# Feeding a float64 weight to a retention + FFN kernel piece by piece, with room for eight pieces, earlier conversions and a new order of the first chunks

## The chip, the cores and the metric

The kernel runs on one core of one Trainium2 chip. A core has a matrix engine (TensorE), a vector engine (VectorE), a scalar engine (ScalarE), a general engine (GpSimd) and an engine that here only issues transfers (SyncE); each works through its own queue in order. The metric is the device time of one execution in microseconds (us). The kernel before takes 979.1 us, the median of three runs (978.93 to 979.91).

## The reference

```python
# attention: q, k, v of shape (8, 8, 576, 64), float32
scores = scale * np.matmul(q, k.transpose(0, 1, 3, 2))
Dmat = np.where(rel >= 0, gamma[:, None, None] ** rel[None, :, :], 0.0)   # decay, one gamma per head
ret = scores * Dmat[None, :, :, :]
attn = np.matmul(ret, v)
# to x of shape (4608, 512), then a feed-forward layer with a squared relu
h = np.maximum(x @ w_in, 0.0)       # w_in  (512, 2048)
out = h * h @ w_out                 # w_out (2048, 512)
```

One thing in the inputs matters here: `w_in` and `w_out` are scaled by a float64 number and so come as float64. [...]the kernel converts both to float32 by integer operations on the two 32-bit words of each number.

## The kernel before

**Tiling.** Tokens are cut into chunks of at most 128 (576 = 4 x 128 + 64, so five chunks for each batch, 40 in all) for the retention, and into nine blocks of 512 for the feed-forward layer. A chunk goes through `turn` (transposes of q and k), `scores`, a masking, and `retain_a`, `retain_b`, `retain_c` (the outputs and the state that is carried from chunk to chunk); its result is copied to `xT`, the transposed input of the feed-forward layer.

**The weights.** `w_in` is cut into 16 pieces of 512 x 128: the list `pieces` holds a 128-wide column block m (0 to 7) and a half e of the hidden dimension. A piece is loaded as float64 (512 KB) into a raw buffer and converted by six steps (`round_parts`): `one` and `two` on VectorE take exponent and high fraction out of the high word (L234, L238), `beside` on ScalarE turns exponent (L242) and low word (L243) into floats, and `three`, `four`, `five` on VectorE put them together (L246, L249, L252). `w_in_parts` lines these steps up, from piece `N_ALONE` on with `one` and `two` of the next piece ahead of `three` of this one; `convert(count)` issues the next `count` of them. Where they are issued is written out by hand, between the parts of the first chunks and then in `ffn`.

**The loads.** The first two pieces are loaded singly (1 KB rows), the rest in pairs (2 KB rows, two neighbouring column blocks) into three pair buffers. `fetch_raw` loads the next ones if there is room; it is called by hand at first, and later by the last step of each conversion. All loads and stores apart from three at the start stand in the one queue of SyncE, in program order, also those of q, k and v and the stores of the hidden values (`g_dram`).

**Block 0.** The first block is multiplied without the Strassen scheme of the others, because it has only the pieces that are converted so far: step j (`first_in`, L699) takes piece j times the 512 tokens (eight matmul instructions of 512 columns), ScalarE applies the relu (L704), and the square (L707) is put into a list from which `some(2)` of a later step issues it on VectorE. The first `N_HALF` pieces are multiplied in two halves: with the first 256 tokens as soon as these are there, and with the other 256 when chunk 3 is done. The last four steps also issue sums of converted pieces for block 1 (L263 to L266). From chunk 5 on the loop calls `ffn(i - 1, 0)` and `ffn(i - 1, 1)`, which issue one, then two steps of block 0 for each chunk with six conversion steps between them. After block 0 the blocks 1 to 8 follow in Strassen form (L735, L1077), paced by the table `PACE`.

**Warm-up.** `warm(n)` (L862) issues matmuls on a constant whose result nobody reads; they keep TensorE occupied while it has no other work.

Of the kernel before, what the change touches and what calls it, by code (L numbers as in the profile page):

```python
# [10 lines left out]
U32 = mybir.dt.uint32  # L11
# [29 lines left out]
def kernel(  # L41
# [91 lines left out]
    def load(i, names="qkv"):  # L133
        b, ci, c0, cs = chunks[i]
        if i == 0:
            nc.sync.dma_start(dv, decays)
        got = loaded.setdefault(i, [None] * 3)
        for name, pool, src in (("q", ld3, q), ("k", ld5, k), ("v", ld4, v)):
            if name not in names:
                continue  # L140
            t = got["qkv".index(name)] = pool.tile([128, H, D], F32, tag=name, name=f"{name}_ld")

            issue = nc.scalar if i == 0 and name != "q" else nc.sync
            at = src[b, :, c0:c0 + cs, :].rearrange("h s d -> s h d")
            if name == "v":
                issue.dma_start(t[:cs], at)
            else:

                for e in range(2):
                    issue.dma_start(t[:cs, e * HP:(e + 1) * HP, :], at[:, e::2, :])  # L150
# [2 lines left out]

    pieces = [(0, 2 * mp + mm, e) for mp in range(N_MP) for e in range(2) for mm in range(2)]
    pieces += [(1, mq + mh * N_MQ, e) for mq in range(N_MQ) for mh in range(2) for e in range(2)]
    N_W1 = N_DF
    N_ALONE = 4
    N_HALF = 2  # L160
    stage = [W[5].rearrange("p (o s f) -> p o s f", o=4, s=NP),
             W[6][:, 0:3 * NP * 128].rearrange("p (o s f) -> p o s f", o=3, s=NP)]
    N_PAIR = 3
    raw_all = [W[4][:, j * 1024:(j + 1) * 1024] for j in range(3)]
    raw_one = [W[4 + j][:, 2048:3072] for j in range(2)]
    raw_two = [W[4 + j][:, 0:2048] for j in range(N_PAIR)]
    exp_all = [W[4 + j][:, 3072:3584] for j in range(3)]
    wide = moe_w_in.dtype != F32

    def raw_of(j):  # L170


        if j >= N_W1:
            return raw_all[(j - N_W1) % 3].rearrange("p (n two) -> p n two", two=2)
        if j < 2:
            return raw_one[j].rearrange("p (c f two) -> p c f two", c=N_DM, two=2)
        t = raw_two[(j // 2 - 1) % N_PAIR].rearrange("p (c m f two) -> p c m f two", c=N_DM, m=2, two=2)
        return t[:, :, j % 2, :, :]

    def exp_of(j):  # L180
        return exp_all[j % 2] if j < N_W1 else exp_all[2 * (j % 2)]
# [4 lines left out]
    def piece_src(j):  # L186
        wi, m, e = pieces[j]
        f = (m + e * N_M) * 128
        return moe_w_out[f:f + 128, :].rearrange("p (c f) -> p c f", c=N_DM)

    def in_src(j, count):
        wi, m, e = pieces[j]
        f = (m + e * N_M) * 128
        return moe_w_in.rearrange("(c p) f -> p c f", p=128)[:, :, f:f + 128 * count]

    def piece_dst(j):
        wi, m, e = pieces[j]
# [5 lines left out]
    def as_dst(j, t):  # L203

        if pieces[j][0] == 0:
            return t
        return t.rearrange("p (o s f) -> p o s f", o=2, s=2)

    def fetch_w(j):
        if j < len(pieces) and wide:  # L210
            to = raw_all[(j - N_W1) % 3].bitcast(I64).rearrange("p (c f) -> p c f", c=N_DM)
            nc.sync.dma_start(to, piece_src(j))

    def fetch_in(j, count):
        if not wide:
            return
        to = (raw_one[j] if count == 1 else raw_two[(j // 2 - 1) % N_PAIR]).bitcast(I64).rearrange("p (c f) -> p c f", c=N_DM)
        nc.sync.dma_start(to, in_src(j, count))

    def round_parts(j):
        first = pieces[j][0] == 0
        at = (lambda t, w: t[:, :, :, w]) if first else (lambda t, w: t[:, :, w])
        lo, hi = (at(raw_of(j).bitcast(U32), w) for w in range(2))
        frac = at(raw_of(j), 0)
        scale = exp_of(j).rearrange("p (c f) -> p c f", c=N_DM) if first else exp_of(j)
        exp = scale.bitcast(U32)
        t = piece_dst(j)  # L230
        bits = t.bitcast(U32)

        def one():
            nc.vector.tensor_scalar(exp, hi, 20, 0x7FF, op0=ALU.logical_shift_right, op1=ALU.bitwise_and)  # L234

        def two():

            nc.vector.tensor_scalar(bits, as_dst(j, hi), 0xFFFFF, 0x100000, op0=ALU.bitwise_and, op1=ALU.bitwise_or)  # L238

        def beside():  # L240

            nc.scalar.activation(exp, exp, AF.Relu, bias=exp_bias[:, 0:1], scale=2.0 ** 23)  # L242
            nc.scalar.activation(frac, lo, AF.Copy, scale=2.0 ** -52)  # L243

        def three():
            nc.vector.scalar_tensor_tensor(t, bits, 2.0 ** -20, as_dst(j, frac), op0=ALU.mult, op1=ALU.add)  # L246

        def four():
            nc.vector.tensor_tensor(t, t, as_dst(j, scale), op=ALU.mult)  # L249

        def five():
            nc.vector.scalar_tensor_tensor(bits, as_dst(j, hi), 0x80000000, bits, op0=ALU.bitwise_and, op1=ALU.bitwise_or)  # L252

        if not wide:
            if pieces[j][0]:
                return [lambda: nc.sync.dma_start(t.rearrange("p o s f -> p (o s) f"), piece_src(j))] + [lambda: None] * 5
            return [lambda: nc.sync.dma_start(t, in_src(j, 1))] + [lambda: None] * 5
        return [one, two, beside, three, four, five]

    def sum_w_in(mp):  # L260
# [51 lines left out]
    def fetch_raw(count):  # L312

        for _ in range(count):
            j = n_raw[0]
            if j < N_W1 and (j < 2 * N_PAIR + 2 or n_made[0] >= j - 2 * N_PAIR + 2):
                count = 1 if j < 2 else 2
                fetch_in(j, count)
                n_raw[0] += count


    def w_in_parts():
# [33 lines left out]
    load(1, "qk")  # L356
    fetch_raw(1)
    load(1, "v")
    load(2)
    fetch_raw(1)  # L360

# [457 lines left out]
    def ffn(i, half):  # L819

        gone[0] += chunks[max(0, min(i, N_CH - 1))][3] / 2
        if half == 2:
            gone[0] += chunks[min(i + 1, N_CH - 1)][3] / 2
        if steps and steps[0][0] == 0:

            move(6)
            for f in (step, lambda: convert(6)) if half else (lambda: convert(6), step):
                f()
            if half and steps and steps[0][0] == 0:
                step()  # L830
                convert(6)
            return
        if not behind:
            behind.append((gone[0] - HALF, done[0]))
        points = behind + [p for p in PACE if p[0] > behind[0][0]]
        want = points[-1][1]
        for (x0, y0), (x1, y1) in zip(points, points[1:]):
            if gone[0] < x1:
                want = y0 + (y1 - y0) * (gone[0] - x0) / (x1 - x0)
                break  # L840
        count = max(1, int(want) - done[0])
        while steps and count:
            held[0] = half != 1 and count <= (1 if half else 2)

            if half == 2:
                due = sum(m[0] <= i + 2 for m in moves)
                move(max(2, min(4, -(-due // (count - 1)))) if count > 1 else 0)
            else:
                move(4 if half and len(moves) > 8 else 3 if half else 2 if count > 1 else 0)
            busy[0] = len(flips) > 0  # L850
            for f in flips[:1]:
                f()
            del flips[:1]
            step()
            count -= 1
        held[0] = busy[0] = False


    def warm(count):
        t = ps_f.tile([128, 512], F32, tag="f", name="idle_ps")  # L860
        for _ in range(count):
            nc.tensor.matmul(t[:, 0:256], lhsT=idle, rhs=idle[:, 0:1].to_broadcast([128, 256]), start=True, stop=True)  # L862
# [17 lines left out]
    turn_in(0, (0,))  # L880
    turn_out(0)
    load(3)
    warm(1)
    scores(0)
    turn(1)
    fetch_raw(1)
    retain_a(0)
    scores(1)
    scale_q(2, nc.gpsimd)
    retain_b(0)  # L890
    retain_c(0)
    load(4)
    fetch_raw(2)
    convert(2)
    warm(1)
    retain_a(1)
    convert(1)
    warm(1)
    retain_b(1)
    retain_c(1)  # L900
    load(5)
    convert(3)
    turn(2, (0, 0))
    warm(2)
    scores(2)
    scale_q(3, nc.gpsimd)
    convert(2)
    first_in(0, (0,))
    retain_a(2)
    convert(1)  # L910
    retain_b(2)
    retain_c(2)
    load(6)
    convert(3)
    first_in(1, (0,))
    turn(3)
    warm(1)
    scores(3)
    scale_q(4, nc.gpsimd)
    convert(3)  # L920
# [1 line left out]
    early.close()  # L922
    ps_t[0] = first.enter_context(tc.tile_pool(name="ps_t", bufs=1, space=PS))
    turn(4)
    convert(3)
    retain_b(3)
    retain_c(3)
    load(7)
    fetch_raw(1)
    step()  # L930
    step()
    scores(4)
    convert(6)
    scale_q(5, nc.gpsimd)
    step()
    convert(6)
    for i in range(N_EARLY + 1, N_CH + 1):
        if i > N_ONE:
            move(C, i)
# [288 lines left out]
```

## Time and profile before

| | before |
|---|---|
| device time, median of 3 | 979.1 us |
| span of the profile | 973.0 us |
| TensorE busy | 951.0 us (98%) |
| VectorE busy | 783.2 us (80%) |
| ScalarE busy | 337.3 us (35%) |
| GpSimd busy | 135.0 us (14%) |
| TensorE's waits over 60 ns to 112 us | 13.4 us in 15 waits |
| `w_in` loads | two of 512 KB, seven of 1024 KB |

The profile comes from one execution, in which a hardware profiler records each instruction's start and end. A line such as `96.74 3.70 PE L699 MATMUL h_ps<-room,w ... x8 [0.17 <-DVE w L252]` reads: at 96.74 us from the start, for 3.70 us, TensorE (PE) ran eight matmuls of source line 699, which write the tile `h_ps` and read `room` and `w`; before them it sat idle for 0.17 us, and what ended this was the VectorE (DVE) instruction of line 252 that writes `w`. ACT is ScalarE, POOL GpSimd, SP SyncE. `PEclk` or "granted clock" is the share of the full TensorE clock that the chip grants.

### The profile page before, as it was taken

The numbers are of one execution on the slowest core, as the hardware profiler recorded it, in microseconds if no ns is written. First come the engines' busy times: TensorE is split into PE (matmuls) and PEld (weight loads), VectorE is DVE, ScalarE is ACT, GpSimd is POOL, SyncE is SP. The second block draws the span as 40 slices with busy tenths as digits, with TensorE's granted clock in tenths as the row PEclk, the third lists the DMA queues.
The fourth block names the chain that finished last, engine by engine and source line by source line (L and its number), as shares of the span: only waits on it lengthen the run. The fifth ranks groups of instructions, "written<-read, shape, count | busy, mean of one in ns | idle before, by whom it ended". The sixth has DMA issues, their size and how long they took to land. (4 is left out here: it accounts for less than half of the span.)

```text
span 973.0 us, 23644 instructions
## 1 busy us (share of the span) xinstructions
PE 951.0 (98%) x10004; PEld 849.6 (87%) x10004; DVE 783.2 (80%) x1445; ACT 337.3 (35%) x808; POOL 135.0 (14%) x121
## 2 busy tenths in 40 slices
PE   8799899999999999999999999999999999999998
PEld 6545588888888888878888899999999999999998
DVE  3698689988889887978876597888888787787876
ACT  3345276765765766656631000000000000000000
POOL 3311143222232122221210000000000000000000
PEclk9999899999999999999999999999999999999999
DMA  9966386686757876766158967445364454524241
GB/s 229 215 201 171 88 202 182 170 258 204 187 158 213 243 190 189 208 199 185 61 223 325 360 245 265 171 158 185 109 206 152 159 193 176 198 100 173 88 174 44
DMA packets 167034, 181.40 MB, mean 186 GB/s; under 512 B 116752, under 2 KB 123920, under 8 KB 160272
## 3 DMA queue, kind: packets, MB, share of 16 engines
q1 hardware_dynamic: 164832, 179.37, 59.3%
q8 instruction: 78, 1.28, 0.5%
q10 hardware_dynamic: 2096, 0.52, 0.2%
q14 instruction: 28, 0.23, 0.1%
HBM read 109.36 MB, written 70.52 MB: 185 GB/s over the span
## 5 line engine op out<-in xcount | busy, mean ns | idle before, releaser
L735 PE MATMUL h_b<-room,w 128*128 128x256 f32 x768 | 183.5, 382 | 2.1 <-DVE room L754 1.8
L438 ACT COPY qk<-flip 32x256 f32<-32x256 f32 x416 | 167.4, 402 | 6.2
L735 PEld LDWEIGHTS h_b<-room,w 128*128 128x128 f32 x768 | 144.2, 190 | 24.0 <-DVE room L754 3.0
L1077 PE MATMUL o_b<-w,room 128*128 128x128 f32 x1168 | 144.4, 275 | 0.2 <-DVE room L1029 0.2
L1077 PEld LDWEIGHTS o_b<-w,room 128*128 128x128 f32 x1168 | 137.2, 192 | 0.4 <-DVE room L1029 0.4
L735 PE MATMUL h_a<-room,w 128*128 128x256 f32 x512 | 122.4, 381 | 2.2 <-issue 2.2
L1077 PE MATMUL o_c<-w,room 128*128 128x128 f32 x1008 | 123.0, 275 | 0.0
L735 PE MATMUL h_c<-room,w 128*128 128x256 f32 x512 | 121.7, 380 | 0.0
L1077 PEld LDWEIGHTS o_c<-w,room 128*128 128x128 f32 x1008 | 117.7, 192 | 0.0
L735 PEld LDWEIGHTS h_a<-room,w 128*128 128x128 f32 x512 | 96.3, 190 | 16.0 <-issue 2.6
L735 PEld LDWEIGHTS h_c<-room,w 128*128 128x128 f32 x512 | 96.7, 190 | 13.3
L1091 ACT COPY r<-o_a 128x128 f32<-128x128 f32 x53 | 14.1, 265 | 271.7 <-PE o_a L1077 236.0
L1077 PE MATMUL o_a<-w,a 128*128 128x128 f32 x688 | 85.7, 275 | 0.0
L752 POOL TENSOR_TENSOR room<-room 128x512 f32<-128x512 f32 x32 | 35.8, 1119 | 337.2 <-ACT room L751 337.2
L1077 PEld LDWEIGHTS o_a<-w,a 128*128 128x128 f32 x688 | 81.2, 192 | 0.1
L742 DVE SCALAR_TENSOR_TENSOR room<-room 128x512 f32<-128x512 f32 x96 | 70.6, 735 | 3.3
L699 PE MATMUL h_ps<-room,w 128*128 128x512 f32 (+1 forms) x144 | 62.0, 577 | 8.6 <-DVE w L252 7.9
L401 POOL TENSOR_TENSOR q_ld<-q_ld,dv 128x512 f32<-128x512 f32 (+1 forms) x39 | 47.3, 1212 | 91.9 <-DMA q_ld<-in_q_dram 91.8
L594 PEld LDWEIGHTS x_ps<-qk,v_ld 64*64 64x64 f32 x1152 | 43.9, 134 | 16.8 <-issue 14.3
L699 PEld LDWEIGHTS h_ps<-room,w 128*128 128x128 f32 x144 | 27.1, 197 | 35.2 <-issue 25.5
L594 PE MATMUL x_ps<-qk,v_ld 64*64 64x64 f32 x1152 | 54.9, 223 | 2.7 <-issue 1.1
L515 POOL TENSOR_TENSOR v_ld<-v_ld,dv 128x512 f32<-128x512 f32 (+1 forms) x40 | 53.0, 1325 | 6.7 <-DMA v_ld<-in_v_dram 6.7
(105 smaller groups left out, 1348.8 us busy)
## 6 DMA issues: line engine op xcount, KB each, us to landing
g_dram<-room SPq DMA_DIRECT2D x32, 1280.0 KB, 5.7
a<-g_dram SPq DMA_DIRECT2D x30, 1024.0 KB, 5.7
room<-g_dram SPq DMA_DIRECT2D x15, 1024.0 KB, 5.8
w<-w_dram SPq DMA_DIRECT2D x7, 1792.0 KB, 9.9
out_dram<-room SPq DMA_DIRECT2D x17, 512.0 KB, 3.3
q_ld<-in_q_dram SPq DMA_DIRECT2D x64, 128.0 KB, 5.6
w<-in_moe_w_out_dram SPq DMA_DIRECT2D x16, 512.0 KB, 4.3
k_ld<-in_k_dram SPq DMA_DIRECT2D x62, 128.0 KB, 5.1
```

The lines of the kernel that those rows point to most:

```text
L401: engine.tensor_tensor(t, t, dv[:cs, :, NCH + ci:NCH + ci + 1].to_broadcast([cs, H, D]), op=ALU.mult)
L438: nc.scalar.copy(*moves.pop(0)[2:])
L515: nc.gpsimd.tensor_tensor(vs[:cs], vs[:cs], dv[:cs, :, ci:ci + 1].to_broadcast([cs, H, D]), op=ALU.mult)
L594: return [lambda hp=hp, e=e, b=b: nc.tensor.matmul(x_at(hp, e, b, h), lhsT=s["vs"][rows(h), head(hp, e), :], rhs=s["ret"][rows(h), e, hp, ...
L699: nc.tensor.matmul(p.rearrange("p h t -> p (h t)"), lhsT=w[:, c, :], rhs=xT[0][:, c, lo * HT:hi * HT], start=(c == 0), stop=(c == N_DM - 1))
L735: nc.tensor.matmul(p[:, mm, :], lhsT=w[:, c, :], rhs=xs[n][right][:, c, :], start=(j in OPENS and mm == 0 and c == 0), stop=(j in CLOSES a ...
L742: nc.vector.scalar_tensor_tensor(t, t, 0.0, t, op0=ALU.max, op1=ALU.mult)
L752: nc.gpsimd.tensor_tensor(g["A11"], g["A11"], g["A11"], op=ALU.mult)
L1077: nc.tensor.matmul(p, lhsT=s["lefts"][left][:, m, :], rhs=w_out[j][:, m, WO_SLOT[right], :], start=(i in OPENS and m == 0), stop=(i in CLO ...
L1091: nc.scalar.copy(r[:, 0, 0:128], p)
```

## The change

The change alters the feeding of `w_in` and the hand-written order of the first chunks:

- Each piece is loaded singly, in 1 KB rows, and there is room for eight raw pieces instead of two single ones and three pairs. The order of the pieces follows: both halves e of a column block come one after the other. A fetch may go out when the piece eight places earlier is converted.
- The loads stand sooner in the queue: the second piece ahead of chunk 2, the third ahead of chunk 3, two more ahead of chunk 4, and three ahead of chunk 5.
- Conversion starts sooner (three steps before `scores(1)`) and runs two pieces ahead of block 0 when the loop begins. `N_ALONE` goes from 4 to 3, and three pieces instead of two are multiplied in halves. Four of the calls of `warm` among the first chunks are left out.
- In `beside`, the low word is converted ahead of the exponent.
- Step 3 of block 0 is issued ahead of the loop; to make up for it, the first chunk of the loop issues one step less.

```diff
-    pieces = [(0, 2 * mp + mm, e) for mp in range(N_MP) for e in range(2) for mm in range(2)]
+    pieces = [(0, m, e) for m in range(N_M) for e in range(2)]
...
-    N_ALONE = 4
-    N_HALF = 2
+    N_ALONE = 3
+    N_HALF = 3
...
-    N_PAIR = 3
-    raw_all = [W[4][:, j * 1024:(j + 1) * 1024] for j in range(3)]
-    raw_one = [W[4 + j][:, 2048:3072] for j in range(2)]
-    raw_two = [W[4 + j][:, 0:2048] for j in range(N_PAIR)]
+    N_RAW = 8
+    raw_all = [W[4 + j // 3][:, (j % 3) * 1024:(j % 3 + 1) * 1024] for j in range(N_RAW)]
...
+            nc.scalar.activation(frac, lo, AF.Copy, scale=2.0 ** -52)
             nc.scalar.activation(exp, exp, AF.Relu, bias=exp_bias[:, 0:1], scale=2.0 ** 23)
-            nc.scalar.activation(frac, lo, AF.Copy, scale=2.0 ** -52)
...
-            j = n_raw[0]
-            if j < N_W1 and (j < 2 * N_PAIR + 2 or n_made[0] >= j - 2 * N_PAIR + 2):
-                count = 1 if j < 2 else 2
-                fetch_in(j, count)
-                n_raw[0] += count
+            if n_raw[0] < min(N_W1, n_made[0] + N_RAW):
+                fetch_w(n_raw[0])
+                n_raw[0] += 1
...
     load(1, "v")
+    fetch_raw(1)
     load(2)
     fetch_raw(1)
...
-            if half and steps and steps[0][0] == 0:
+            if half and i > N_EARLY and steps and steps[0][0] == 0:
...
     load(3)
+    fetch_raw(2)
     warm(1)
     scores(0)
     turn(1)
-    fetch_raw(1)
     retain_a(0)
+    convert(3)
     scores(1)
     scale_q(2, nc.gpsimd)
     retain_b(0)
     retain_c(0)
     load(4)
-    fetch_raw(2)
+    fetch_raw(3)
     convert(2)
-    warm(1)
     retain_a(1)
-    convert(1)
-    warm(1)
+    convert(4)
     retain_b(1)
     retain_c(1)
     load(5)
     convert(3)
-    turn(2, (0, 0))
-    warm(2)
+    first_in(0, (0,))
+    turn(2)
+    convert(3)
+    first_in(1, (0,))
     scores(2)
     scale_q(3, nc.gpsimd)
+    retain_a(2)
     convert(2)
-    first_in(0, (0,))
-    retain_a(2)
-    convert(1)
     retain_b(2)
     retain_c(2)
     load(6)
+    convert(1)
+    turn(3)
     convert(3)
-    first_in(1, (0,))
-    turn(3)
-    warm(1)
+    first_in(2, (0,))
     scores(3)
     scale_q(4, nc.gpsimd)
     convert(3)
...
     turn(4)
-    convert(3)
+    convert(2)
     retain_b(3)
     retain_c(3)
     load(7)
-    fetch_raw(1)
     step()
     step()
     scores(4)
     convert(6)
     scale_q(5, nc.gpsimd)
     step()
-    convert(6)
+    convert(3)
+    step()
+    convert(3)
```

More of the change, by code (lines that the diff above doesn't have):

```diff
@@ L170, in raw_of @@
     def raw_of(j):
[L173 to L178, printed above, removed]
+        return raw_all[j % N_RAW] if j < N_W1 else raw_all[(j - N_W1) % 3]
     def exp_of(j):
@@ L188, in piece_src @@
         f = (m + e * N_M) * 128
+        if wi == 0:
+            return moe_w_in.rearrange("(c p) f -> p c f", p=128)[:, :, f:f + 128]
         return moe_w_out[f:f + 128, :].rearrange("p (c f) -> p c f", c=N_DM)
[L191 to L194, printed above, removed]
     def piece_dst(j):
@@ L205, in as_dst @@
         if pieces[j][0] == 0:
-            return t
+            return t.rearrange("p (c f) -> p c f", c=N_DM)
         return t.rearrange("p (o s f) -> p o s f", o=2, s=2)
@@ L210, in fetch_w @@
         if j < len(pieces) and wide:
[L211 to L218, printed above, removed]
-    def round_parts(j):
[L224 to L229, printed above, removed]
+            nc.sync.dma_start(raw_of(j).bitcast(I64).rearrange("p (c f) -> p c f", c=N_DM), piece_src(j))
+    def round_parts(j):
+        words = raw_of(j).bitcast(U32).rearrange("p (n two) -> p n two", two=2)
+        lo, hi = words[:, :, 0], words[:, :, 1]
+        frac = raw_of(j).rearrange("p (n two) -> p n two", two=2)[:, :, 0]
+        exp = exp_of(j).bitcast(U32)
         t = piece_dst(j)
@@ L248, in four @@
         def four():
-            nc.vector.tensor_tensor(t, t, as_dst(j, scale), op=ALU.mult)
+            nc.vector.tensor_tensor(t, t, as_dst(j, exp_of(j)), op=ALU.mult)
         def five():
@@ L254, in round_parts @@
         if not wide:
-            if pieces[j][0]:
-                return [lambda: nc.sync.dma_start(t.rearrange("p o s f -> p (o s) f"), piece_src(j))] + [lambda: None] * 5
-            return [lambda: nc.sync.dma_start(t, in_src(j, 1))] + [lambda: None] * 5
+            to = t if pieces[j][0] == 0 else t.rearrange("p o s f -> p (o s) f")
+            return [lambda: nc.sync.dma_start(to, piece_src(j))] + [lambda: None] * 5
         return [one, two, beside, three, four, five]
```

## The prediction

> **What bounds the kernel now.** I read the stages first: TensorE's busy time by ten microseconds (stretch and length; busy us and instructions of TensorE, its weight loads, VectorE, ScalarE and GpSimd; granted clock; DMA share and GB/s).
>
> ```profile
> 30.00:40.00 10.00, 7.87 (x166) 6.42 (x161) 5.87 (x11) 3.42 (x8) 3.38 (x4) 1.00 0.92 223
> ...
> 60.00:70.00 10.00, 9.21 (x98) 4.41 (x98) 9.32 (x14) 5.30 (x11) 2.86 (x2) 1.00 0.83 210
> ...
> 100.00:110.00 10.00, 7.44 (x49) 3.65 (x48) 5.71 (x7) 1.34 (x3) 2.93 (x3) 0.66 0.07 27
> ...
> 140.00:150.00 10.00, 9.91 (x163) 8.56 (x162) 9.86 (x16) 6.91 (x16) 2.17 (x2) 1.00 0.29 82
> ```
>
> From 120 us on TensorE is full; over the whole span it is busy 951.0 of 973.0 us. What can be won lies in the first 112 us: the loads (DMA share near 1 to 45 us) and block 0, where VectorE, which converts `w_in` from doubles, is nearly as full as TensorE. The waits of TensorE to 125 us (total, times, longest) name the reason:
>
> ```profile
> PE h_ps L699 <- DVE w L252: 7.9, 7, 2.6
> ...
> PE x_ps L594 <- DVE qk L506: 1.0, 1, 1.0
> ...
> PE h_ps L699 <- ACT room L571: 0.7, 1, 0.7
> ```
>
> L252 is a conversion's last operation: TensorE waits seven times for a piece of `w_in`. The timeline of TensorE has the worst, piece 15:
>
> ```profile
> 96.74 3.70 PE L699 MATMUL h_ps<-room,w 128*128 128x512 f32 x8 [0.17 <-DVE w L252]
> ...
> 104.26 6.53 PE L699 MATMUL h_ps<-room,w 128*128 128x512 f32 x8 [2.56 <-DVE w L252]
> ```
>
> The same eight matmuls take 3.70 us in every other step and 6.53 here, since the clock was 0.50 from 103.16 to 109.98 us. So this wait cost 2.56 + 2.83 = 5.4 us. VectorE's timeline tells why piece 15 was late:
>
> ```profile
> 95.99 0.69 DVE L252 SCALAR_TENSOR_TENSOR w<-w,w 128x512 uint32<-128x512 uint32 x1
> 98.40 0.69 DVE L246 SCALAR_TENSOR_TENSOR w<-w,w 128x512 f32<-128x512 uint32 x1 [1.71 <-ACT w L243]
> 99.00 1.54 DVE L707 TENSOR_TENSOR room<-room 128x512 f32<-128x512 f32 x1
> 100.47 1.54 DVE L265 TENSOR_TENSOR w<-w 128x512 f32<-128x512 f32 x1
> 101.94 1.54 DVE L249 TENSOR_TENSOR w<-w,w 128x512 f32<-128x512 f32 x1
> 103.51 0.69 DVE L252 SCALAR_TENSOR_TENSOR w<-w,w 128x512 uint32<-128x512 uint32 x1
> ```
>
> L252 of piece 14 ends at 96.7. VectorE then waits 1.71 us for ScalarE, whose two conversions stand behind the Relu of step 13. Next come a square and a sum that belong to step 14, and only then L249 and L252 of piece 15; three operations take 1.54 us instead of 0.69 while GpSimd scales `v` (2.96 us at 99.96).
>
> **What the Trainium skill says.** "TensorE: Matmul & The Clock Gate", Part 1: the array runs at half rate after an idle window of about 3.4 us, in a free-running window of 3413 ns, and at full rate again after a busy one. The trace agrees on the period: 4.17 to 103.16 is 29.0 windows and the drop lasts 2.0. It does not agree that the window must be idle, as the windows below show. The same page (Architectural detail) has ScalarE and VectorE strictly FIFO; the chain above behaves so. "SBUF — State Buffer", Who interferes with whom: a VectorE operation with two SBUF inputs contends with a GpSimd one that reads SBUF; 0.69 against 1.54 agrees. "DMA: Bandwidth & Descriptors", Specifications, asks for 512 B or more per transfer for line rate; so single pieces (1 KB) should not be much worse than pairs (2 KB). In the trace a 1 KB packet took 51 to 53 ns in the median, a 2 KB one 84 to 89.
>
> **The change part by part.**
>
> (1) *Lead of the conversions.* Counting the steps handed to `convert`: before, 90 of 98 stand ahead of steps 12 and 13, 96 ahead of 14, and the last two (L249, L252 of piece 15) come after step 14. After: 92, 92, 98. So at the tightest places the lead grows from 4 to 6 operations, and piece 15's end is ahead of step 14's square and sum. It would run 98.4, 99.0, 99.7 on the old clock and end near 100.4, or 101.7 if GpSimd still meets it; step 14 ends at 100.4 and its small matmuls at 101.7. So the wait and the clock drop go: 5.4 us. The four smaller waits of the same kind between 50 and 97 us (0.17, 0.70, 0.79, 0.17) go too: 1.8 us.
>
> (2) *Does VectorE carry it?* From 45.07 to 104.26 us TensorE is busy 54.8 us of 59.2, VectorE 52.7, and VectorE waits 5.9 us for L243 (seven waits). It must end 3.9 us sooner for TensorE to run unbroken. It starts this stretch about one piece further on (2.6 us, from L234 of one piece to L234 of the next without waits), and with the fraction converted first, L246 need not wait for ScalarE's other operation (0.62 us from start to start, seven times, 4.3 us at most). 2.6 plus some of 4.3 is enough, by little. I take back 1.0 us for waits that stay (bounds 0 and 3.9).
>
> (3) *The first four chunks.* On landings: `w_in`'s second piece now goes ahead of chunk 2, a third ahead of chunk 3, two ahead of chunk 4. A piece needs 1.5 to 1.9 us (512 packets of 53 ns on 16 engines, and `v` of chunk 1 landed 1.2 us after the piece ahead of it), so `q` of chunk 2 lands near 14.5 instead of 12.4, `v` of chunk 3 near 23.3 instead of 21.3, `v` of chunk 4 near 30.5 instead of 29.2; chunk 5 as before within 1 us, since eight pieces are ahead of it in both. Their matmuls start later than that (retention of chunk 3 at 31.5 before), so no load ends a wait in my chain:
>
> ScalarE's copy of chunk 1 ends at 17.8; first half of step 0 (1.99) to 19.8; transposes of chunk 2 (0.7) to 20.5; first half of step 1 (1.97) to 22.5; scores (0.9) to 23.4; the masking is now bare (0.9, like the 0.99 at 31.48) to 24.3; retention (2.5, as 21.67 to 24.15) to 26.8; transposes (0.7) to 27.5; first half of step 2 (1.97) to 29.5; scores and mask (1.8) to 31.3; from there to the first second half 3.7 (31.48 to 35.20) to 35.0; two halves (3.7) to 38.7; scores (0.6), third half (1.9), step 3 (3.6), transposes of chunk 5 (0.8) to 45.6. The old kernel has the same work done at 48.7: 3.1 us won. The warm-up matmuls removed (3.2 us) filled idle time and give nothing back.
>
> (4) *The clock between 11 and 25 us.* Here I use the windows of 3.41 us that the clock events mark:
>
> ```profile
> 14.41:17.82 3.41, 2.76 (x91) 2.23 (x90) 0.64 (x1) 2.25 (x5) 1.15 (x2) 1.00 1.12 263
> ...
> 24.65:28.06 3.41, 1.67 (x8) 1.44 (x8) 1.86 (x4) 0.40 (x2) 0.54 (x1) 1.00 1.12 231
> ...
> 99.74:103.16 3.42, 1.96 (x42) 1.13 (x40) 3.42 (x3) 1.34 (x3) 3.19 (x3) 1.00 0.24 84
> ```
>
> The window that cost the clock had 1.96 us busy, 1.26 of it small matmuls of the retention; 1.67 us of dense ones did not. The first of the three loses 0.74 us of warm-up and 0.7 of transposes and would have some 1.35 us, all small. I expect the clock to drop near 17.8 and to come back after one full window: 3.41 us at half speed, 1.7 us lost (bounds 0 and 3.4).
>
> (5) *Small things.* Seven more DMA issues at about 0.4 us on SyncE, whose queue has room; the fetches of pieces 8 to 15 go out when five to eight pieces are made, and their old data are long read. Singles cost 0.4 us of transfer more per two pieces, beside other work. After block 0 the program is the same, and TensorE is full.
>
> Sum: 3.1 - 1.7 + 1.8 + 5.4 - 1.0 = 7.6 us; 979.1 - 7.6 = 971.5.
>
> **The rivals.** A: the clock holds in the early part (full rate from 4.17 to 103.16 in the old profile speaks for it, the windows against): 9.3 us, 969.8. B: VectorE is the bound at the end of block 0; the cycle from 87.67 to 104.26 has 14.70 us of VectorE against 13.86 of TensorE, so piece 15 is late again and the clock drops there. Only 3.1 - 1.7 + 1.8 and some 0.6 of the last wait are won: 975.3. Against it: the lead carries over from the cycles before, where VectorE has 12.1 of 13.5. C, slower: the later loads do end waits (2 us lost where I won 3.1), the early clock drop lasts two windows (3.4), and of the 7.2 us of waits only half go: +1.8, 980.9. DMA near 1.0 to 45 us speaks for it; chunk 3's 8 us of slack against.
>
> **How the numbers follow.** Forecast 0.44, A 0.29, B 0.14, C 0.13. The range leaves out C and the best of A: 967.5 to 976.5. Faster 0.86, the same 0.03 (between B and C), slower 0.11.
>
> **What would show it.** Step 15 starts within 1 us of the matmuls before it and takes 3.7 us at clock 1.00; L249 and L252 of piece 15 stand ahead of the square of step 13 or 14. The waits of L699 for L252 fall from 7.9 to under 2 us. Step 4 starts near 45.6 to 47.5 (old: 50.5). A half-rate window shows near 18 to 21 us. I am wrong if the early chain waits for `q`, `k` or `v`, if that drop lasts longer, or if VectorE reaches 100% in block 0 and TensorE still waits.

## The result, and the profile after

The changed kernel takes 967.7 us (median of 4 runs, 967.0 to 970.1) against 979.5 us of the kernel before in the same session: a ratio of 0.9882, 95% interval 0.9862 to 0.9902. The forecast was 971.5, with a range of 967.5 to 976.5. In the sessions of the experiments the kernel before had medians of 977.3 to 978.9 over 11 to 37 runs, so the gain is nearer 10 than 12 us (e5, which takes as long as the changed kernel, was 10.0 us under the kernel before in its own session).

The spans of the two profiles are 973.0 and 966.2 us. The waits of TensorE in the first 125 us come first (who waited for whom; total, times, longest, in us):

```profile
PE x_ps L571 <- issue: 2.5, 1, 2.5
PE x_ps L571 <- DVE qk L483: 2.5, 3, 1.0
...
PE h_ps L676 <- issue: 0.9, 1, 0.9
...
PE h_ps L676 <- DVE w L231: 0.3, 1, 0.3
```

Lines 676 and 231 are the old 699 and 252. The 7.9 us of waits for converted pieces are down to 0.3. What stands on top is new: "issue", a wait for nothing that the profile shows, and the masking (L483). The end of block 0 on TensorE, and piece 15 on VectorE, answer to the lines shown of before:

```profile
93.24 7.13 PE L676 MATMUL h_ps<-room,w 128*128 128x512 f32 x16
101.57 3.70 PE L676 MATMUL h_ps<-room,w 128*128 128x512 f32 x8
```

```profile
98.17 0.69 DVE L225 SCALAR_TENSOR_TENSOR w<-w,w 128x512 f32<-128x512 uint32 x1 [1.43 <-ACT w L221]
98.96 0.69 DVE L228 TENSOR_TENSOR w<-w,w 128x512 f32<-128x512 f32 x1
99.69 0.69 DVE L231 SCALAR_TENSOR_TENSOR w<-w,w 128x512 uint32<-128x512 uint32 x1
100.30 1.55 DVE L684 TENSOR_TENSOR room<-room 128x512 f32<-128x512 f32 x1
```

Steps 13 and 14 run back to back, and step 15 starts without a wait and takes 3.70 us where it took 6.53. Piece 15 is done at 100.4, ahead of the square that GpSimd slows to 1.55 us. The early part looks otherwise. Here are two lines of TensorE, and then its windows between clock events (stretch, length; busy us of TensorE, weight loads, VectorE, ScalarE, GpSimd; clock; DMA share, GB/s):

```profile
17.05 0.26 PE L571 MATMUL x_ps<-qk,v_ld 64*64 64x64 f32 x1 [2.54 <-issue]
...
20.66 3.78 PE L676 MATMUL h_ps<-room,w 128*128 128x256 f32 x8 [0.67 <-ACT room L548]
```

```profile
12.68:16.09 3.41, 0.99 (x42) 0.72 (x31) 3.27 (x6) 1.21 (x3) 1.36 (x2) 1.00 1.31 227
16.09:19.50 3.41, 1.98 (x62) 1.79 (x65) 1.30 (x3) 1.55 (x3) 1.06 (x1) 0.50 0.97 253
19.50:22.92 3.42, 2.75 (x25) 2.13 (x18) 1.75 (x3) 0.86 (x2) 1.47 (x1) 0.50 0.85 178
22.92:26.33 3.41, 3.41 (x22) 2.41 (x21) 0.77 (x2) 1.19 (x3) 1.06 (x1) 0.50 1.16 307
47.23:101.57 54.34, 54.34 (x634) 27.98 (x632) 47.45 (x79) 26.72 (x50) 7.74 (x7) 1.00 0.62 176
```

After a window with 0.99 us of work the clock is at half for three windows, and step 0's first half takes 3.78 us in place of 1.99. Step 3 and the transposes behind it end at 51.4 us; the old kernel had come as far at 48.7. From there TensorE is full without a break (last line). So the first 51 us lost 2.7 us, and the stretch to the end of block 0 won 8.2 (62.1 against 53.9), which puts the end of block 0 at 105.3 where it was at 110.8. The rest, from there to the end of the span, took 862.2 us before and 860.9 after.

### The profile page after: what moved, and what is told of

Same layout as the page of the kernel before. It is cut to its first block, busy times and chain, and to the rows that moved or that the text cites. A ratio compares the mean times of both kernels' runs of the same rounds, so it can differ in the third digit from the quotient of the medians.

```text
span 966.2 us, 23674 instructions
## 1 busy us (share of the span) xinstructions
PE 948.0 (98%) x10002; PEld 851.0 (88%) x10002; DVE 783.2 (81%) x1447; ACT 338.0 (35%) x808; POOL 134.4 (14%) x121
## 5 line engine op out<-in xcount | busy, mean ns | idle before, releaser
L729 POOL TENSOR_TENSOR room<-room 128x512 f32<-128x512 f32 x32 | 35.9, 1121 | 336.4 <-ACT room L728 336.4
L571 PEld LDWEIGHTS x_ps<-qk,v_ld 64*64 64x64 f32 x1152 | 44.3, 135 | 19.4 <-issue 16.1
L676 PEld LDWEIGHTS h_ps<-room,w 128*128 128x128 f32 x152 | 29.1, 199 | 24.4 <-issue 19.6
```

Of the source, the lines that this page charges most:

```text
L571: return [lambda hp=hp, e=e, b=b: nc.tensor.matmul(x_at(hp, e, b, h), lhsT=s["vs"][rows(h), head(hp, e), :], rhs=s["ret"][rows(h), e, hp, ...
L676: nc.tensor.matmul(p.rearrange("p h t -> p (h t)"), lhsT=w[:, c, :], rhs=xT[0][:, c, lo * HT:hi * HT], start=(c == 0), stop=(c == N_DM - 1))
L729: nc.gpsimd.tensor_tensor(g["A11"], g["A11"], g["A11"], op=ALU.mult)
```

## The experiments

Five rounds each, beside runs of the kernel before on the same chip; the ratio compares with those. Where two altered kernels are compared below, their medians can come from different sessions and chips, so such differences can be off by 2 or 3 us.

| run | median us (runs) | ratio to before, 95% interval |
|---|---|---|
| e1 kernel before again | 977.2 (22) | 0.9997, 0.9984 to 1.0010 |
| e2 changed, three warm-ups put back | 962.3 (5) | 0.9853, 0.9834 to 0.9872 |
| e3 before, with the lead alone | 972.1 (7) | 0.9960, 0.9932 to 0.9988 |
| e4 changed, without the lead | 974.1 (15) | 0.9964, 0.9947 to 0.9980 |
| e5 changed, exponent first | 967.6 (5) | 0.9895, 0.9874 to 0.9915 |
| e6 new feeding alone | 976.1 (14) | 0.9985, 0.9971 to 0.9999 |
| e7 e2, second piece behind chunk 2 | 963.4 (5) | 0.9849, 0.9825 to 0.9874 |
| e8 e2, scores ahead of the half steps | 962.8 (4) | 0.9847, 0.9823 to 0.9870 |
| e9 before, wait for piece 15 filled | 972.2 (10) | 0.9951, 0.9935 to 0.9967 |
| e10 before, four warm-up calls left out | 976.8 (22) | 0.9988, 0.9974 to 1.0002 |
| e11 e7 with three parts moved | 963.7 (4) | 0.9862, 0.9839 to 0.9885 |
| e12 changed, four matmuls at 47 us | 969.0 (6) | 0.9901, 0.9878 to 0.9925 |

**e1: how steady is the kernel before?** No edit.

> The kernel before, unchanged, to see clock and span of several of its executions: its profile had a span of 973.0 us at a mean clock of 0.996, but its timed runs take 979 us. Theory (the free-running activity windows fall differently in each execution): executions near 973 us with one clock drop of 6.8 us, and others near 978 us with further or longer drops, at clocks of 0.990 or less. Rival (the profiled execution is simply not comparable): all spans near 978 us at the same clock of 0.996.

Its 22 executions span 972.5 to 978.4 us, at mean clocks of 0.998 down to 0.990. In the profiled one (977.3 us) the clock fell four times: 25.7 to 32.5, 35.9 to 42.7, 107.6 to 111.0 and 428.4 to 431.9 us. In the profile that the prediction rested on it fell once. All drops are whole windows of 3.41 us, and the window grid stands elsewhere in each execution. The theory holds as far as this shows it: one program, the same order, and up to 6 us between executions. The eight with a mean clock of 0.996 or more have spans of 972.5 to 975.6 us, the six with 0.991 or less 976.4 to 978.4. That it is the place of the grid which decides is read from two profiles only. The profile of before was one of the better executions, 2 us below the mean span of 975.3.

**e3 and e4: the lead of the conversions, alone and taken away.**

```diff
 # e3, on the kernel before
     step()
-    convert(6)
+    convert(8)
 # e4, on the changed kernel
     step()
-    convert(3)
+    convert(1)
```

> The kernel before with two more conversion steps ahead of the loop (8 in place of 6), nothing else: the lead at steps 12 to 14 is then that of the changed kernel. Theory (the lead alone removes the waits for L252 and the clock drop at 103 us): 6 to 7.5 us faster than before, ratio 0.993. Rival (the gain needs the pieces loaded and converted sooner): under 2 us faster, ratio 0.998 or more.

> The changed kernel with two conversion steps fewer ahead of the loop (1 in place of 3), so that the lead is that of the kernel before; loads, buffers and order of the first chunks as changed. Theory (lead): the waits of block 0 for L231 come back, that for piece 15 with a clock drop, 5 to 7 us slower than the changed kernel, ratio 0.994. Rival (loads and early order): as fast as the changed kernel, ratio 0.988.

Two conversion steps more make the old kernel 5.4 us faster by the medians, 3.9 by the ratio (interval 1.2 to 6.6); two fewer make the changed one 6.4 us slower, which leaves 3.4 us against the kernel before for all the rest of the change. The end of block 0 in e3 and in e4:

```profile
93.84 7.13 PE L699 MATMUL h_ps<-room,w 128*128 128x512 f32 x16
102.16 3.70 PE L699 MATMUL h_ps<-room,w 128*128 128x512 f32 x8
```

```profile
86.98 3.70 PE L676 MATMUL h_ps<-room,w 128*128 128x512 f32 x8 [0.47 <-DVE w L231]
...
107.75 3.70 PE L676 MATMUL h_ps<-room,w 128*128 128x512 f32 x8 [1.83 <-DVE w L231]
```

In e3 step 15 follows without a wait; in e4 the waits for L231 are back, 3.4 us of them behind step 3 where the changed kernel has none, though not the clock drop at step 15 in this execution. From the end of step 3 (52.7 us in e4, 50.8 in the changed kernel, ahead of the transposes) to its own end, block 0 takes 58.7 us in e4 and 54.5 in the changed kernel. In the kernel before it takes 62.1, or 59.2 without what the slow clock costs step 15. So in block 0 nearly the whole gain goes with the lead. (e4's profile was also 1.9 us later at the end of step 3, where the two programs are still the same; that is not the lead's.) e3 falls a little short of the 6 to 7.5 us expected, since two smaller waits for L252 (0.8 us each at 73.6 and 88.0) stayed and scores waited for a copy on VectorE (1.5 us at 50.0): with the lead alone VectorE is still a little late in the middle, and block 0 takes 57.8 us from step 3 on. The lead removes the waits fully only together with the rest of the change.

**e9: what a wait costs beside its length.**

```diff
 # the kernel before
                 turn(i)
+            if i == N_EARLY + 5:
+                warm(4)
             move(C, i)
```

> The kernel before with four warm-up matmuls just ahead of step 15, in the 2.6 us in which TensorE waits for piece 15; the wait itself stays. Theory (the wait has two costs, 2.6 us of idle time and a clock drop that a sparse window brings): no drop after 100 us, and the mean 1.5 to 3 us under the kernel before (the drop is one or two windows of 3.4 us, at half speed). Rival (the drop comes with any wait, or the clock is hidden there): no difference, under 0.7 us.

```profile
104.70 2.01 PE L862 MATMUL idle_ps<-w 128*128 128x256 f32 x8
107.44 3.67 PE L699 MATMUL h_ps<-room,w 128*128 128x512 f32 x8 [0.73 <-DVE w L252]
```

The wait is about as long as before (2.7 us), now filled for 2.0 us of it, and step 15 runs at full clock. The gain was 5.2 us and so more than expected. The trace has a reason for the surplus, another gap: the old kernel idles on "issue" for 2.2 us at 425.9 us, and e9 has no such gap. In the profiles of e1, e3 and e6, which have it too, it lay mostly in one window, left 1.1 to 1.7 us of work there, and a clock drop of one window followed. So between 2 and 4 us of the 5.2 (an estimate: the gap, and half a window) may have nothing to do with the wait for piece 15. See e12.

**e2 and e10: the warm-up matmuls.**

```diff
 # e2, on the changed kernel
     convert(2)
+    warm(2)
     retain_a(1)
     convert(4)
+    warm(1)
     retain_b(1)
 ...
     convert(3)
+    warm(1)
     first_in(0, (0,))
```

> The changed kernel with warm-up matmuls put back into three idle places between 12.7 and 20.7 us (two calls ahead of the retention of chunk 1, one inside it, one ahead of step 0). Theory (the clock dropped at 16 us because that window was sparse, and cost about 3 us): no drop before 110 us, 2 to 3.5 us faster than the changed kernel, ratio to the kernel before 0.985. Rival (the early part is bound by loads and instruction fetch, the clock is hidden): within 0.7 us of the changed kernel, ratio 0.988.

> The kernel before without the four calls of warm that the change leaves out (ahead of the retention of chunk 1, inside it, and ahead of the scores of chunks 2 and 3). Theory (these matmuls filled idle time but held the clock): a drop between 14 and 18 us in every execution, 2 to 5 us slower than before, ratio 1.003 or more. Rival (they only cost time, and the drops have other causes): the same or up to 1.5 us faster.

e2 is 5.4 us faster than the changed kernel by the medians (2.8 by the two ratios, 4.1 by the ratio of e5) and has the lowest median of all. Its executions ran at mean clocks of 0.996 to 1.000, those of the changed kernel at 0.991 to 0.995. In the one profiled the clock still fell once, at 16.2, for two windows in place of three; block 0 ended at 102.2 in place of 105.3. e10 went against the expected time: it is as fast as the kernel before. Its clock did what the theory says (mean 0.990 over 22 executions against 0.994; a drop at 17.4 us behind a window with 1.32 us of work), and block 0 ended at 117.1 us in its profile against 110.8 and 113.2. But here too the gap near 426 us had gone, and the stretch behind block 0 took 859.8 us in place of 862.2. With the gap moved at the same time, e10 does not tell what the four calls are worth.

**e12: the gap at 420 us.**

```diff
 # the changed kernel, ahead of the loop
     convert(3)
+    warm(4)
```

> The changed kernel with four warm-up matmuls just ahead of the loop, at 47 us, where TensorE is full and its clock is not in question: the same number of added instructions as in the run with three warm-ups put back. Theory (TensorE's idle time of 2.0 us near 420 us is an instruction fetch whose place depends on how many instructions stand ahead of it): that gap goes or shrinks to 0.7 us, which gives back the 1.7 us that the four matmuls cost; within 0.7 us of the changed kernel (967.7), with the clock drop at 16 us as before. Rival (the gap has to do with the state of block 5 there, and the warm-ups gave all of the 5.4 us through the clock): the gap stays at 1.8 to 2.3 us and the kernel takes 1.7 us more, 969.4.

In the changed kernel the gap reads:

```profile
419.82 1.35 PE L712 MATMUL h_a<-room,w 128*128 128x256 f32 x5 [1.99 <-issue]
```

In e12 it is gone, TensorE is full from 410 to 440 us, and there is one of 0.49 us at 361 us instead. Over all 14 profiles the gap goes by the number of matmul instructions: 10002 or 10004 give 1.8 to 2.3 us between 419 and 428 us (7 profiles), 10010 give 0.5 to 0.7 near 355 (5), 9994 and 10012 none over 0.15 us. So its place depends on how many instructions stand ahead.

That it is an instruction fetch the DMA records show. Every profile has 78 packets of 16 KB of instructions; in the changed kernel one runs from 417.20 to 418.27 us, and the gap ends 1.55 us after it. The same holds for all 35 idle times on "issue" over 0.12 us in the 14 profiles: each ends 1.3 to 1.8 us after such a packet. And each stands at a fixed place in the count of TensorE's instructions (matmuls, weight loads and semaphore operations): in the changed kernel 449, 961 and 10434 stand ahead of the three gaps, and in all 35 cases the count leaves 193 to 195 when divided by 256. Why one of these boundaries shows a gap and another none stays open.

The stretch behind block 0 fell from 860.9 us to 859.3 in e12 and 859.4 in e2, so about 1.5 us of e2's gain come from here; the rest is the clock and the early part. The gap itself went as the theory says. The median, 969.0, is nearer the rival's number; in this profile a second early drop, at 37.8 us (e4's profile has one too), used up what was won, and six runs (965.6 to 971.4) don't settle the sum.

**e7: the other gap, at 14 to 17 us.**

```diff
 # e2, and
     load(1, "v")
-    fetch_raw(1)
     load(2)
-    fetch_raw(1)
+    fetch_raw(2)
```

> The run with three warm-ups put back (962.3 us), but the load of the second piece behind chunk 2's again, as in the kernel before. Theory (TensorE's idle time near 14 to 17 us, of 2.0 us there, is an instruction fetch that queues behind the loads in front of it): the 16 KB packet of the fetch starts near 12.3 in place of 13.9 us and the gap falls to 1.2 us or less, while step 1 may come later for its piece lands at 18 us. Rival (the gap has another cause): it stays within 0.3 us of 2.0.

The 16 KB packets of instructions run through the same DMA engines as the data. The first such packet starts at 13.9 us in e2, and TensorE resumes at 16.5 after 1.98 us; in e7 it starts at 11.5, and this is left of the gap:

```profile
14.39 0.21 PE L564 MATMUL u_ps<-v_ld,k_ld 64*64 64x64 f32 x1 [0.20 <-issue]
19.31 1.99 PE L675 MATMUL h_ps<-room,w 128*128 128x256 f32 x8 [2.10 <-ACT room L547]
```

So the gap is the fetch, and moving one load moves it: it queues behind the loads. Over all 14 profiles the gap grows with the start of that packet, if not strictly: up to 0.45 us for starts of 11.5 to 11.8 us (3 profiles), 0.5 to 1.1 for 12.3 to 12.9 (5), 1.4 to 2.5 for 13.7 to 14.3 (6). In its profile e7 ran at full clock throughout, and yet it won no time against e2: the second line shows the new wait, ScalarE's copy of chunk 1's result behind its conversion of piece 1, whose load now landed later.

**e8 and e11: attempts to take the next wait away.**

```diff
 # e8: e2, and the same for scores(3) and first_in(2, (0,))
-    first_in(1, (0,))
     scores(2)
     scale_q(3, nc.gpsimd)
+    first_in(1, (0,))
 # e11: e7, with the first of these two moves, and
     retain_a(1)
-    convert(4)
+    convert(1)
     warm(1)
     retain_b(1)
     retain_c(1)
     load(5)
-    convert(3)
+    convert(6)
```

> The run with three warm-ups put back, with the scores of chunks 2 and 3 ahead of the half steps 1 and 2 in place of behind them, so that the masking on VectorE (1.0 us of wait twice) lies beside those matmuls. Theory (these waits are on TensorE's path): 1.5 to 2.2 us faster than 962.3, ratio to the kernel before 0.983. Rival (VectorE or the loads set the pace of the first 40 us): within 0.5 us of 962.3.

> The run with three warm-ups and the second piece behind chunk 2 (963.4 us), with ScalarE's conversion of piece 1 moved behind its copy of chunk 1's result, and the scores of chunk 2 ahead of step 1's first half. Theory (in that run TensorE stood 2.1 us ahead of step 0 because ScalarE, in order, waited for piece 1's load ahead of that copy): step 0 starts near 17.3 in place of 19.3 us, 1.5 to 2.5 us faster than 963.4, about 961. Rival (another wait, for piece 1 or for the masking, takes its place): within 0.7 us of 963.4.

Both rivals held: 962.8 and 963.7, no better than e2. In e8 the two waits for the masking are gone and scores wait for ScalarE instead (0.7 and 1.3 us), and a gap on "issue" of 2.0 us stands at 35.7 us. In e11 step 0 starts at 18.1 us, but a gap of 1.8 us on "issue" stands ahead of step 2's first half. As far as these two runs show, the first 40 us have several chains of nearly the same length.

**e5 and e6: the other parts by themselves.** e5 swaps the two `nc.scalar.activation` lines of `beside` back. e6 has the new pieces, buffers and single loads with the old order of work; `fetch_raw` asks there for as many pieces as the old pairs held.

> The changed kernel with the two ScalarE conversions in the old order (exponent first). Theory (the order frees VectorE by 0.6 us for each wait on ScalarE, and the lead makes up for it): within 1 us of the changed kernel, L225 waits longer for ScalarE, but TensorE still does not wait for L231. Rival (this order is what lets VectorE keep up): waits of step 8, 11 or 14 for L231 come back, 1.5 to 5 us slower than the changed kernel.

> The new feeding alone: single pieces, room for eight, new order of the pieces, but every load, conversion and step of the first chunks in the old places, four pieces alone, two halves, exponent first. Theory (single loads cost little and bring little by themselves, the order of the work does it): within 1.5 us of the kernel before, ratio 0.999 to 1.001, with the wait for piece 15 as before. Rival (room for eight is the gain): 4 us or more faster, ratio under 0.996.

The order on ScalarE gives nothing: 967.6 against 967.7, and VectorE waits 5.4 us in place of 5.2 for it between 44 and 112 us. The feeding alone gives about 1.5 us (0.9985, interval 0.9971 to 0.9999, that is 0.1 to 2.8 us), with the wait for piece 15 at 2.57 us. It is not itself the gain; whether the new order could do without it was not tried.

## Why the prediction was right, and where its steps were off

*Step 1, the lead: right.* No wait for a piece is left in block 0 from step 3 on; 7.2 us were forecast. e3 and e4 show it from both sides, with 3.9 to 5.4 and with 6.4 us (4.3 in the profiles' block 0), and step 15 at 3.67 us in e9 shows that the wait's cost was in part the clock. How much that part is differs between executions: 2.83 us in the profile of before, 1.4 in e1's.

*Step 2, VectorE carries it: right, and 1.0 us too careful.* The waits that I took back did not stay: TensorE is busy 54.34 of 54.34 us. One of its two supports did no work, since e5 shows the order of ScalarE's conversions without effect. The other, that VectorE starts this stretch further on, seems to have been needed: e3, which has the lead but not the sooner conversions, kept 1.6 us of waits for L252 in this stretch and 2.0 us in which scores waited for VectorE.

*Step 3, the first four chunks: the step that failed.* I had 3.1 us won, before the clock. Together with step 4 the sum was +1.4, and the profile shows -2.7. The loads did land where I put them (`q` of chunk 2 at 14.5, `v` of chunk 3 at 23.0, of chunk 4 at 30.6 us), and none ended a wait of the matmuls. The failed term is the one I took over unchanged: that ScalarE's copy of chunk 1 ends at 17.8 us. It ended at 20.6. The first two lines are of before, the third is of after:

```profile
15.06 0.27 PE L594 MATMUL x_ps<-qk,v_ld 64*64 64x64 f32 x2 [1.13 <-issue]
17.24 0.58 ACT L571 COPY room<-x_ps 128x512 f32<-128x512 f32 x1
20.03 0.59 ACT L548 COPY room<-x_ps 128x512 f32<-128x512 f32 x1 [0.89 <-PE u_ps L565]
```

Of these 2.8 us half is the instruction fetch, which was in the profile of before as 1.13 us of "issue" and which I held for fixed: the piece put ahead of chunk 2 delayed it, and the gap grew to 2.54 us (e7 shows the cause). Of the rest, 0.6 us were lost ahead of the gap and 0.8 behind it, at half clock. A second fetch gap of 0.95 us came at 35.6.

*Step 4, the clock: right in kind, too small.* The drop came close to where the window count had put it, at 16.1 in place of 17.8, but the window was emptier (0.99 us, not 1.35) because of that fetch, and the clock stayed down for three windows, not one. e4, e5 and e12, whose early order is the same, had the drop too, at 17.35 to 17.58 us and for two windows, and e4 and e12 another two windows at 37.8 or 37.9. By the prediction's own sign ("if that drop lasts longer") this step was wrong in its size. Still the forecast's branch and not rival A came true, though A's 969.8 us was the nearer number. What A assumed, a full clock throughout, is seen only in the profiles of e7 and e11, with warm-up matmuls put back; their medians are 963.4 and 963.7 us.

*What balanced these.* Steps 1 and 2 gave 8.2 us in the profile where 6.2 were forecast: 7.2 of waits and of clock, and 0.8 because three pairs of steps that a wait had split now run as one, in 7.13 us in place of twice 3.70. The stretch behind block 0 gave 1.3 us where I had none. So the profiles differ by 6.8 us where 7.6 were forecast, but by luck: errors of -4.1, +2.0 and +1.3 us nearly cancel. The timed runs of the old kernel lose more to the clock than its profile does (e1), so that 6.8 us between the profiles are some 10 between medians. Against the first comparison the forecast was 4 us too small, and the measured time lies only 0.2 us inside its range.

*Rival B* fell: VectorE had 47.45 of 54.34 us. Of *rival C* the loads ended no waits of the matmuls, but its longer clock drop came, with three windows where it had two.

What stays open: what exactly the clock counts (see the last section), and how what e2 has beyond the gap at 420 us divides between the clock and the early order. An order of the first 40 us without both the fetch's gap and the waits that replaced it was not found.

## What to carry to other kernels

Where a producer and a consumer engine are nearly equally busy, count how many producer operations stand ahead of each consumer step, and look for the step where the producer's last operation is queued behind work that belongs to a later step: two operations of lead were worth some 4 to 6 us here. A matmul that fills idle time looks free to remove, but weigh the window that it stands in: three such calls put back won 3 to 5 us (e2), of which about 1.5 came from the fetch gap at 420 us. When an edit adds or removes instructions, look whether such a gap far away has come or gone before crediting the edit with the time. And take several executions of the kernel before into account: here one and the same program varied by 6 us.

## What the runs showed of the hardware that was not expected

- The half-rate clock follows from a sparse window, not only an idle one. Of the windows of 3.41 us at full clock that begin before 960 us in the 14 profiles, every one with up to 1.54 us of matmuls was followed by a drop. Between that and 2.3 us some were (1.96 us in the kernel before, 2.27 in e9) and some were not (1.67 in the kernel before, 1.98 in e7), and above it none was. So the busy time that the profiler shows is not quite what counts. At half clock, all 18 windows with 3.4 us of work brought the full clock back at their end; of the 17 with 1.98 to 3.11 us only three did. The drop of the changed kernel fits this: its three windows had 1.98, 2.75 and 3.41 us. The Trainium skill ("TensorE: Matmul & The Clock Gate", Part 1) speaks of an idle window; the measurement decides. The grid's phase moves from execution to execution (first event at 4.17 us in one profile, 5.85 in another).
- TensorE's instructions come in 16 KB packets, 78 in each profile, through the same DMA engines as the data; one takes 1.0 us in the median and about 1.3 us among the loads near 14 us. Where TensorE then idles, it does so until 1.3 to 1.8 us after the packet has ended, and always at the same place in every 256 instructions. So loads put sooner can delay instructions. Eight to ten matmuls more or fewer were enough that in place of a gap of 2 us near 420 us there was one of 0.5 to 0.7 us some 65 us earlier, or none.
